# A gated attention and MLP decode step: 832 columns of w2 placed on partitions 0 to 63 by eight small transfers, where 384 columns went to partitions 0 to 15 by four

## The chip, the cores and the metric

The kernel runs on one core of a Trainium2 chip, in one launch. The metric is device microseconds of a whole execution, the median of the runs shown; lower is better. The profile is one further execution, recorded by the hardware profiler, and its own time (its span) is shorter than the timed runs, because the span begins with the first instruction and ends with the last.

## The reference

One decode step for two tokens (B = 2, D = 576). An attention branch A with a KV cache of 4096 positions and 32 heads of 128, an MLP branch with 4608 hidden units and a tanh gelu, and a gate that mixes the two, all in float32:

```python
x = A_x                                               # (2, 1, 576)
g = _sigmoid((x * gate_w).sum(-1, keepdims=True))

q = (x @ wq).reshape(B, 1, 32, 128).transpose(0, 2, 1, 3)
scores = einsum("bhqd,bhkd->bhqk", q, k_cache) * 128 ** -0.5    # k_cache (2, 32, 4096, 128)
p = softmax(scores)
o = einsum("bhqk,bhkd->bhqd", p, v_cache)
a = o.transpose(0, 2, 1, 3).reshape(B, 1, 4096) @ wo            # wo (4096, 576)

h = gelu(x @ w1 + b1)                                 # w1 (576, 4608)
b = h @ w2 + b2                                       # w2 (4608, 576)

out = g * a + (1 - g) * b
```

Nearly all of the 308 MB that is read is the two caches.

## The kernel before, in words

**Storage.** One tile of SBUF, `ring` (128 partitions, three slots of 16,384 words each), takes every large transfer. At the start wq and w1 lie in it; after that slot after slot is refilled in the order k0, v0, k1, v1, ..., k15, v15 (each 8 MB, four heads of one token, 64 KB to each partition) and at the end three mixed loads, the list `LAST`. `load_next` issues the next transfer as soon as the oldest slot is free: a k slot after the scores of it are reduced (the last reader is DVE, `red`; the release is written after `max_n`, L522 in the profile's waits), a v slot after its matmuls (PE, `av`, L551). All of these transfers are issued by SP, strictly in the order of the program. A few small ones (x, gate_w, b1, b2) are issued by ACT.

**The loop.** For each of 16 groups of four heads: DVE multiplies k by the broadcast q (`mul`, L512) and reduces (`red`, L516 on POOL for a part, L517 and L518 on DVE), ACT takes the exponentials (L537), PE multiplies with v (L551), DVE and PE fold the result (L562, L568).

**The tail.** The MLP's second product and the output projection are done at the end. `h` is held as `hg`, 128 partitions by 36 rows, so that partition p, row r is hidden unit 36p + r, and the row r of w2 in the layout "(p r) n" is 128 partitions by 576 columns. `mlp_out(lo, hi)` multiplies rows lo to hi - 1 of it into the accumulator `acc` (`acc_mm`, L371: two products of 288 columns for each row; the profile records each float32 product as two MATMULs). `wo_out` does the same with rows of wo, and `last_out` does rows 23 to 31 of wo into `res` (L463, L487), adds `acc` (L473), copies out and issues the store (L493).

**The columns set apart.** The last 384 of each partition's 36 x 576 words of w2 (the end of row 35) don't lie with the rest on 128 partitions. Before, four transfers (`wx`, L156) put them on partitions 0 to 15: each takes 4 partitions, and each partition receives eight runs of 384 words, which come from eight different partitions p of the layout. `mlp_x` multiplies them with `hx`, a copy of the matching values of `hg` on 16 partitions, made by small products with columns of the identity (L417, L421). `LAST` says which load holds what: rows of w2, the columns set apart (`"wx"`), rows of wo. The last rows of wo come in ever smaller transfers, row 31 in three pieces. The third load is seven transfers in all, the last before the store.

**Order of completion counters.** In the program as built, the transfers use eight completion counters in turn (SP's and ACT's together), and a transfer whose counter is still in use waits at its issue until the transfer eight places before it has landed.

Of the kernel before, what the change touches and what calls it, by code (L numbers as in the profile page):

```python
# [8 lines left out]
F32 = mybir.dt.float32  # L9
# [10 lines left out]
def kernel(  # L20
# [14 lines left out]
    nc = tc.nc  # L35
    B, H, SK, DH = k_cache.shape
    D = x.shape[-1]
# [16 lines left out]
    F4 = F // NG  # L54
# [3 lines left out]
    NF = F // P  # L58
# [5 lines left out]
    SLOTS = 3  # L64

    LAST = (
        (("w2", 0, 14), ("w2", 14, 28)),
        (("w2", 28, 36), ("wx", 0, 1), ("wo", 0, 15)),
        (("wo", 15, 23), ("wo", 23, 27), ("wo", 27, 30), ("wo", 30, 31), ("wo", 31, 32)),
    )  # L70
    FOLD = 23
    SLOT = R * DH
# [8 lines left out]
    cp = ctx.enter_context(tc.tile_pool(name="cp", bufs=1))  # L81
# [8 lines left out]
    ps_sm = ctx.enter_context(tc.tile_pool(name="ps_sm", bufs=3, space=bass.MemoryType.PSUM))  # L90
# [8 lines left out]
    kt, vt, wqt, w1t, rows = {}, {}, {}, {}, {}  # L99
# [22 lines left out]
    def slot(n):  # L122
        k = len(held) % SLOTS
        return ring[:, k * SLOT:k * SLOT + n]
# [7 lines left out]

    srcs = {"w2": w2.rearrange("(p r) n -> p (r n)", r=NF), "wo": wo.rearrange("(p r) n -> p (r n)", r=32)}

    XE, XC, XW = 4, 4, 384
    XL = D - XW
    XP = XE * XC
    XS = P // XP
    srcx2 = w2.rearrange("(e c s r) n -> c r e s n", e=XE, c=XC, s=XS)[:, NF - 1, :, :, XL:]

    def length(w, a, z):
        return XS * XW if w == "wx" else (z - a) * D - (XW if (w, z) == ("w2", NF) else 0)

    def load_last(m):
        n = sum(length(*q) for q in LAST[m])

        used["e"], used["z"] = len(held) % SLOTS * SLOT + n, (len(held) % SLOTS + 1) * SLOT
        t = slot(n)
        o = 0
        for w, a, z in LAST[m]:  # L150
            if w == "wx":
                xt = t[:XP, o:o + XS * XW]
                rows[w] = xt.rearrange("p (s n) -> p s n", s=XS)
                o += XS * XW
                for c in range(XC):
                    nc.sync.dma_start(xt[c::XC].rearrange("e (s n) -> e s n", s=XS), srcx2[c])  # L156
                continue
            if (w, z) == ("w2", NF):
                nc.sync.dma_start(t[:, o:o + length(w, a, z)], srcs[w][:, a * D:z * D - XW])
                for r in range(a, z):  # L160
                    rows[w, r] = t[:, o + (r - a) * D:o + min((r - a + 1) * D, length(w, a, z))]
                o += length(w, a, z)
                continue

            ends = (a * D, a * D + DS, a * D + DS + DO, z * D) if (w, z) == ("wo", 32) else (a * D, z * D)
            for u, v in zip(ends, ends[1:]):
                nc.sync.dma_start(t[:, o:o + v - u], srcs[w][:, u:v])
                o += v - u
            for r in range(a, z):
                rows[w, r] = t[:, o - (z - r) * D:o - (z - r - 1) * D]  # L170

    def temp(n, parts=P):
        t = ring[:parts, used["t"]:used["t"] + n]
        used["t"] += n
        assert used["t"] <= SLOTS * SLOT
        return t
# [7 lines left out]
    def load():  # L184
        if not seq:
            return
        kind, i = seq.pop()
        if kind == "wq":
            wqt[i] = load_w(wq, ROWS[kind], i)
        elif kind == "w1":  # L190
            w1t[i] = load_w(w1, ROWS[kind], i)
        elif kind == "k":
            kt[i] = load_heads(k_cache, i)
        elif kind == "v":
            vt[i] = load_heads(v_cache, i)
        else:
            load_last(i)
        if kind in ("k", "v", "last"):
            held.append((kind, i))
# [7 lines left out]
    xg = temp(D, B + 1)  # L207
# [8 lines left out]
    def load_b1(ends):  # L216
        to, src = b1r.rearrange("(g q) n -> g q n", g=NG)[:, B], b1.rearrange("(g n) -> g n", g=NG)
        for u, v in zip(ends, ends[1:]):
            nc.scalar.dma_start(to[:, u:v], src[:, u:v])


    load_b1((0, 232))
    for b in range(B):
        nc.scalar.dma_start(xg[b:b + 1], x[b])
    nc.scalar.dma_start(xg[B:B + 1], gate_w[None, :])
    load()
    load()
# [2 lines left out]
    ident = cp.tile([P, P], F32, name="ident")  # L230
# [9 lines left out]
    for j in range(NPB):  # L240
        t = cp.tile([P, NT * 32 + EB], F32, name=f"p{j}")
# [71 lines left out]
    for m, ps in enumerate(qps):  # L313
        nc.scalar.copy(qrow[:, m * 512:(m + 1) * 512], ps)
    nc.scalar.dma_start(b2r, b2[None, :])
    load_b1((232, 464, 696, 928, F4))

# [44 lines left out]
    def acc_mm(lhsT, rhs, k, start=False, stop=False, lo=0):  # L364
        m = lhsT.shape[-1]
        hi = lo + rhs.shape[-1]
        for s in range(NS):
            o = 64 * (k % 2) + 32 * s
            u, v = max(lo, s * DS), min(hi, (s + 1) * DS)
            if u < v:  # L370
                nc.tensor.matmul(  # L371
                    acc[o:o + m, u - s * DS:v - s * DS], lhsT, rhs[:, u - lo:v - lo],
                    start=start, stop=stop, skip_group_check=True,
                )
# [28 lines left out]
    hg = cp.tile([P, NF, B], F32, name="hg")  # L403
    t = temp(NF * B).rearrange("p (r b) -> p r b", b=B)
# [7 lines left out]

    load()

    hxps = ps_sm.tile([XP, XS, B], F32, tag="sm", name="hxps")
    for s in range(XS):
        nc.tensor.matmul(  # L417
            hxps[:, s], ident.rearrange("p (q s) -> p s q", s=XS)[:, s], hg[:, NF - 1], start=True, stop=True
        )
    hx = cp.tile([XP, XS, B], F32, name="hx")  # L420
    nc.scalar.copy(hx, hxps)  # L421

    def mlp_x():
        for s in range(XS):
            acc_mm(hx[:, s], rows["wx"][:, s], s, lo=XL)

    def mlp_out(lo, hi):
        for r in range(lo, hi):
            acc_mm(hg[:, r], rows["w2", r], r)
# [14 lines left out]
    def wo_out(lo, hi):  # L444
        for r in range(lo, hi):
            acc_mm(oP[:, :, r], rows["wo", r], r)
# [178 lines left out]
    o_turn(turn)  # L625
    mlp_out(20, 24)
    mlp_x()
    mlp_out(24, NF)
    wo_out(0, FOLD)
    last_out()  # L630

# [27 lines left out]
```

## Time and profile before

| | |
|---|---|
| median of 3 runs | 721.66 us (721.61 to 721.81) |
| span of the profiled execution | 719.7 us |
| DVE, PE, POOL, ACT busy | 71%, 31%, 20%, 6% of the span |
| packets of SP's queue (q1) | 7060, 99.2% of the time of 16 DMA engines |
| packets of ACT's queue (q10) | 48, 0.0% |
| packets of instruction loads (q8) | 13, 0.1% |
| bytes moved, mean rate | 308.83 MB, 429 GB/s |
| the four transfers of L156, in SP's queue | issued from 682.39 us on, in 2.84 us |
| PE on them (L371, out of `hx`) | 32 MATMULs, 4.01 us from 698.94 us on |
| the store of the result issued (L493) | 717.46 us |

How to read it: the shares of busy time are means over the whole span, and the kernel has an opening (projections), a loop and a tail with different limits. The DMA share of a window is the mean over 16 DMA engines of the time that their packets took; over short windows it swings around 1, so that only a lasting fall says that some of the engines have run out of work. PEclk is the granted clock of TensorE, 1.0 or 0.5 here.

### The profile page before, as it was taken

What the parts mean: (1) busy time and instruction counts of PE and PEld (TensorE: products, weight loads), DVE (VectorE), ACT (ScalarE), POOL (GpSimd) and SP (SyncE); (2) the same over time, 40 slices, a digit from 0 to 9 for tenths busy, and PEclk for the clock granted to TensorE, in tenths of its full rate; (3) what the DMA queues carried; (4) which work ended last, traced back from release to release, by engine and by line L of the source; (5) the groups of instructions that cost most, each with busy time, mean ns of one, the idle gap of its engine ahead of it and who ended that gap; (6) DMA issues with size and microseconds to landing.
All of it is one profiled execution on the core that took longest, in us unless ns stands there. A gap on an engine that the chain in (4) does not pass through costs nothing.

```text
span 719.7 us, 3913 instructions
## 1 busy us (share of the span) xinstructions
PE 223.4 (31%) x1663; PEld 66.1 (9%) x1663; DVE 512.0 (71%) x137; ACT 40.0 (6%) x156; POOL 145.0 (20%) x35
## 2 busy tenths in 40 slices
PE   0675022040514050404133140405060503214198
PEld 0321000010101010101000010101010100000024
DVE  0004969779695969596969879696959695988910
ACT  0110010100001010101010100001010101010000
POOL 2000130404050403022040404040403122040400
PEclk9967557565757575655756575757565665657588
DMA  9999999999999999999999999999999999999997
GB/s 408 412 443 434 426 444 419 455 416 455 416 444 428 426 441 430 438 430 444 430 434 426 441 430 437 431 433 437 437 434 441 423 431 437 430 441 431 420 424 308
DMA packets 7126, 308.83 MB, mean 429 GB/s; under 512 B 810, under 2 KB 1342, under 8 KB 1604
## 3 DMA queue, kind: packets, MB, share of 16 engines
q1 hardware_dynamic: 7060, 308.55, 99.2%
q8 instruction: 13, 0.21, 0.1%
q14 instruction: 5, 0.04, 0.0%
q10 hardware_dynamic: 48, 0.03, 0.0%
HBM read 308.57 MB, written 0.00 MB: 429 GB/s over the span
## 4 chain that ended last, share of the span: by engine, by line
DMA 45%; DVE 35%; PE 17%; ACT 1%; issue 1%; ACTq 0%; POOL 0%; DVEq 0%; POOLq 0%
DMA ring<-in_A_k_cache_dram 39%; DVE ring L512 19%; PE av L551 10%; DVE s L517 10%; DVE s L518 5%; DMA ring<-in_B_w_dram 4%; PE acc L371 3%; DMA ring<-in_gate_w_dram 3%; PE oall L568 2%; PE qps L304 1%; DVE avs L562 1%; PE res L463 0%; ACT p L537 0%; DVE m L522 0%; PE zps L280 0%
## 5 line engine op out<-in xcount | busy, mean ns | idle before, releaser
L512 DVE TENSOR_TENSOR ring<-ring,q 128x16384 f32<-128x16384 f32 x16 | 275.6, 17225 | 110.1 <-DMA ring<-in_A_k_cache_dram 110.1
L516 POOL TENSOR_TENSOR ring<-ring 128x3968 f32<-128x3968 f32 x16 | 137.0, 8565 | 491.3 <-DVE ring L512 491.3
L551 PE MATMUL av<-ring,p 128*32 128x512 f32 x1024 | 141.6, 715 | 167.6 <-ACT p L537 167.6
L517 DVE TENSOR_REDUCE s<-ring 128x66 f32<-128x8448 f32 x16 | 143.2, 8953 | 1.3
L568 PE MATMUL oall<-avs,pick 128*64 128x512 f32 x16 | 14.8, 1028 | 195.1 <-DVE avs L562 167.7
L518 DVE TENSOR_REDUCE s<-ring 128x62 f32<-128x3968 f32 x16 | 68.4, 4277 | 0.1
L551 PEld LDWEIGHTS av<-ring,p 128*32 128x32 f32 x1024 | 36.0, 129 | 278.8 <-issue 220.6
L537 ACT ACTIVATE p<-s,bs 32x128 f32<-32x128 f32 x64 | 25.5, 398 | 479.9 <-DVE bs L531 478.7
L352 PE MATMUL qb<-qm,spread 64*128 64x512 f32 x8 | 8.3, 1138 | 71.4 <-POOL qm L348 71.4
L395 DVE TENSOR_TENSOR ring<-hps,ring 128x384 f32<-128x384 f32 x3 | 1.7, 559 | 32.2 <-PE hps L304 32.0
L371 PE MATMUL acc<-ring,hg 128*2 128x288 f32 (+1 forms) x142 | 14.4, 561 | 25.3 <-DMA ring<-in_B_w_dram 25.3
L568 PEld LDWEIGHTS oall<-avs,pick 128*64 128x64 f32 x16 | 2.2, 196 | 201.9 <-DVE avs L562 201.9
L284 DVE TENSOR_SCALAR gb<-gb 128x2 f32<-128x2 f32 x1 | 0.2, 169 | 24.4 <-ACT gb L283 24.4
L483 DVE COPY ring<-res 2x144 f32<-2x144 f32 x1 | 0.3, 296 | 19.3 <-PE res L463 19.3
L304 PE MATMUL hps<-ring 128*32 128x384 f32 x120 | 12.8, 596 | 0.0
L562 DVE TENSOR_TENSOR avs<-av,selr 128x512 f32<-128x512 f32 x8 | 5.5, 682 | 10.1 <-PE av L551 10.1
L348 POOL TENSOR_TENSOR qm<-qall,mine 64x512 f32<-64x512 f32 x4 | 4.1, 1035 | 40.3 <-ACT qall L331 40.3
L537 ACT ACTIVATION_READ_ACCUMULATOR p<-s,bs 32x1 f32 x64 | 11.8, 184 | 0.0
L304 PE MATMUL qps<-ring 128*32 128x512 f32 x80 | 10.7, 697 | 0.0
L271 PE MATMUL xps<-ident,ring 3*128 3x3 f32 x10 | 1.5, 254 | 23.8 <-DMA ring<-in_gate_w_dram 22.8
L352 PEld LDWEIGHTS qb<-qm,spread 64*128 64x128 f32 x8 | 2.0, 308 | 74.5 <-POOL qm L348 74.5
L354 ACT COPY q<-qb 128x512 f32<-128x512 f32 x4 | 2.3, 585 | 106.3 <-PE qb L352 106.3
(88 smaller groups left out, 79.5 us busy)
## 6 DMA issues: line engine op xcount, KB each, us to landing
ring<-in_B_w_dram SPq DMA_DIRECT2D x2, 4608.0 KB, 34.3
ring<-in_B_w_dram SPq DMA_DIRECT2D x2, 4032.0 KB, 28.6
ring<-in_A_wo_dram SPq DMA_DIRECT2D x1, 4320.0 KB
ring<-in_A_wo_dram SPq DMA_DIRECT2D x1, 2304.0 KB, 22.4
ring<-in_B_w_dram SPq DMA_DIRECT2D x1, 2112.0 KB
ring<-in_B_w_dram SPq DMA_DIRECT2D x1, 1152.0 KB
ring<-in_A_wo_dram SPq DMA_DIRECT2D x1, 1152.0 KB
ring<-in_A_wq_dram SPq DMA_DIRECT2D x1, 1024.0 KB
```

The costliest lines, as they stand in the source:

```text
L304: nc.tensor.matmul(ps[32 * j:32 * j + 32, :width], lhs, ts[c][:, o:o + width], start=(k == 0), stop=last, skip_group_check=True,)
L348: nc.gpsimd.tensor_mul(t, qall.unsqueeze(1).to_broadcast([NO, NQ, DH]), mine[:, u[0]:u[-1] + 1].unsqueeze(2).to_broadcast([NO, NQ, DH]),)
L352: nc.tensor.matmul(ps, spread, t.rearrange("p u d -> p (u d)"), start=True, stop=True)
L371: nc.tensor.matmul(acc[o:o + m, u - s * DS:v - s * DS], lhsT, rhs[:, u - lo:v - lo], start=start, stop=stop, skip_group_check=True,)
L512: nc.vector.tensor_mul(kt[i], kt[i], qs[i].unsqueeze(1).to_broadcast([P, R, DH]))
L516: nc.gpsimd.tensor_add(t[:, :, :DH2], t[:, :, :DH2], t[:, :, DH2:])
L517: nc.vector.tensor_reduce(st[i][:, HALVED:], kt[i][:, HALVED:], AX.X, ALU.add)
L518: nc.vector.tensor_reduce(st[i][:, :HALVED], t[:, :, :DH2], AX.X, ALU.add)
L537: nc.scalar.activation(p[w, :, e * RB:(e + 1) * RB], st[i][w].rearrange("p (t c) -> p t c", c=RB), AF.Exp, bias=bias[i][w], accum_out=rs[w ...
L551: nc.tensor.matmul(ps[32 * j:32 * j + 32], p[:, 32 * t + EB * (1 - half):32 * t + EB * (1 - half) + 32], vt[i][:, RB * t:RB * (t + 1)].rea ...
L562: nc.vector.tensor_mul(t, avs[i].rearrange("p (r d) -> p r d", d=DH), selr.unsqueeze(2).to_broadcast([P, RB, DH]))
L568: nc.tensor.matmul(oall, pick[:, NO - G - i * G:2 * NO - G - i * G], avs[i].rearrange("p r d -> p (r d)"), start=(i == 0), stop=(i == N // ...
```

## The change

Three things change.

- **832 columns instead of 384.** The columns set apart are now the last 832 words of each partition (the last 256 columns of row 34 and the whole of row 35). They go to partitions 0 to 63 in two halves of 32 partitions (`XH = 2`), each half in four transfers (`XC = 4`) of 8 partitions (`XE = 8`); every partition receives two runs of 832 words (`XS = 2`), placed 1024 words apart (`XT`). `hx` has 64 partitions and is made by two products instead of eight; `mlp_x` has three products for each of the two runs instead of two for each of eight. The products on row 35 in `mlp_out` go, those on row 34 have 320 columns.
- **Order of the last loads.** The first half goes out after w2's rows 0 to 13, the second after rows 14 to 23, both in the first of the three last loads; rows 24 to 35 (less 832 words) and rows 0 to 15 of wo are the second load; the third begins at row 16 of wo.
- **Small transfers of ACT.** x's two rows come in one transfer, and b1 in four pieces (232, 308, 308 and 304 columns of each of four groups) instead of five.

```diff
     LAST = (
-        (("w2", 0, 14), ("w2", 14, 28)),
-        (("w2", 28, 36), ("wx", 0, 1), ("wo", 0, 15)),
-        (("wo", 15, 23), ("wo", 23, 27), ("wo", 27, 30), ("wo", 30, 31), ("wo", 31, 32)),
+        (("w2", 0, 14), ("wx", 0, 1), ("w2", 14, 24), ("wx", 1, 2)),
+        (("w2", 24, 36), ("wo", 0, 16)),
+        (("wo", 16, 23), ("wo", 23, 27), ("wo", 27, 30), ("wo", 30, 31), ("wo", 31, 32)),
     )
...
-    XE, XC, XW = 4, 4, 384
-    XL = D - XW
-    XP = XE * XC
+    XE, XC, XH, XR, XL = 8, 4, 2, 2, 320
+    XQ = XE * XC
+    XP = XH * XQ
     XS = P // XP
-    srcx2 = w2.rearrange("(e c s r) n -> c r e s n", e=XE, c=XC, s=XS)[:, NF - 1, :, :, XL:]
+    XW = XR * D - XL
+    XT = 1024
+    srcx2 = w2.rearrange("(s h e c r) n -> h c e s (r n)", s=XS, h=XH, e=XE, c=XC)[:, :, :, :, NF * D - XW:]
...
             if w == "wx":
-                xt = t[:XP, o:o + XS * XW]
-                rows[w] = xt.rearrange("p (s n) -> p s n", s=XS)
-                o += XS * XW
+                if a == 0:
+                    rows[w] = t[:XP, o:o + XS * XT].rearrange("p (s n) -> p s n", s=XS)[:, :, :XW]
                 for c in range(XC):
-                    nc.sync.dma_start(xt[c::XC].rearrange("e (s n) -> e s n", s=XS), srcx2[c])
+                    nc.sync.dma_start(rows[w][a * XQ + c:z * XQ:XC], srcx2[a, c])
+                o += length(w, a, z)
                 continue
...
-    for b in range(B):
-        nc.scalar.dma_start(xg[b:b + 1], x[b])
+    nc.scalar.dma_start(xg[:B], x.rearrange("b s d -> (b s) d"))
     nc.scalar.dma_start(xg[B:B + 1], gate_w[None, :])
...
-    load_b1((232, 464, 696, 928, F4))
+    load_b1((232, 540, 848, F4))
...
-    hxps = ps_sm.tile([XP, XS, B], F32, tag="sm", name="hxps")
+    hxps = ps_sm.tile([XP, XS, XR, B], F32, tag="sm", name="hxps")
     for s in range(XS):
         nc.tensor.matmul(
-            hxps[:, s], ident.rearrange("p (q s) -> p s q", s=XS)[:, s], hg[:, NF - 1], start=True, stop=True
+            hxps[:, s], ident[:, s * XP:(s + 1) * XP], hg[:, NF - XR:], start=True, stop=True
         )
...
     def mlp_x():
         for s in range(XS):
-            acc_mm(hx[:, s], rows["wx"][:, s], s, lo=XL)
+            for r in range(XR):
+                lo, u, v = XL * (r == 0), r * D - XL * (r > 0), (r + 1) * D - XL
+                acc_mm(hx[:, s, r], rows["wx"][:, s, u:v], s + r, lo=lo)
...
     mlp_x()
-    mlp_out(24, NF)
+    mlp_out(24, NF - XR + 1)
```

More of the change, by code (lines that the diff above doesn't have):

```diff
@@ L133 @@
     srcs = {"w2": w2.rearrange("(p r) n -> p (r n)", r=NF), "wo": wo.rearrange("(p r) n -> p (r n)", r=32)}
-    XE, XC, XW = 4, 4, 384
-    XL = D - XW
-    XP = XE * XC
+    XE, XC, XH, XR, XL = 8, 4, 2, 2, 320
+    XQ = XE * XC
+    XP = XH * XQ
     XS = P // XP
-    srcx2 = w2.rearrange("(e c s r) n -> c r e s n", e=XE, c=XC, s=XS)[:, NF - 1, :, :, XL:]
+    XW = XR * D - XL
+    XT = 1024
+    srcx2 = w2.rearrange("(s h e c r) n -> h c e s (r n)", s=XS, h=XH, e=XE, c=XC)[:, :, :, :, NF * D - XW:]
     def length(w, a, z):
-        return XS * XW if w == "wx" else (z - a) * D - (XW if (w, z) == ("w2", NF) else 0)
+        if w == "wx":
+            return XS * XT if a == 0 else 0
+        return (z - a) * D - (XW if (w, z) == ("w2", NF) else 0)
     def load_last(m):
@@ L159, in load_last @@
                 nc.sync.dma_start(t[:, o:o + length(w, a, z)], srcs[w][:, a * D:z * D - XW])
-                for r in range(a, z):
+                for r in range(a, z - XR + 1):
                     rows[w, r] = t[:, o + (r - a) * D:o + min((r - a + 1) * D, length(w, a, z))]
@@ L413 @@
     load()
-    hxps = ps_sm.tile([XP, XS, B], F32, tag="sm", name="hxps")
+    hxps = ps_sm.tile([XP, XS, XR, B], F32, tag="sm", name="hxps")
     for s in range(XS):
         nc.tensor.matmul(
-            hxps[:, s], ident.rearrange("p (q s) -> p s q", s=XS)[:, s], hg[:, NF - 1], start=True, stop=True
+            hxps[:, s], ident[:, s * XP:(s + 1) * XP], hg[:, NF - XR:], start=True, stop=True
         )
-    hx = cp.tile([XP, XS, B], F32, name="hx")
+    hx = cp.tile([XP, XS, XR, B], F32, name="hx")
     nc.scalar.copy(hx, hxps)
```

## The prediction

> **What bounds the kernel now.** I read the page's shares and DMA queues first, then the chain that ended last, then the tail in windows of half a microsecond, then what SP waited for.
>
> ```profile
> span 719.7 us, 3913 instructions
> DMA  9999999999999999999999999999999999999997
> GB/s 408 412 443 434 426 444 419 455 416 455 416 444 428 426 441 430 438 430 444 430 434 426 441 430 437 431 433 437 437 434 441 423 431 437 430 441 431 420 424 308
> DMA packets 7126, 308.83 MB, mean 429 GB/s; under 512 B 810, under 2 KB 1342, under 8 KB 1604
> q1 hardware_dynamic: 7060, 308.55, 99.2%
> q8 instruction: 13, 0.21, 0.1%
> q10 hardware_dynamic: 48, 0.03, 0.0%
> ```
>
> The 16 DMA engines are busy in every slice but the last, SP's queue alone fills 99.2% of their time, and no slice between the second and the last falls out of the swing between 416 and 455 GB/s. The kernel is a stream of 308.83 MB at 429 GB/s, 26.8 GB/s for each engine (429/16). The chain says DMA 45% and names DVE and PE for much of the rest, but it goes through them only because a finished slot releases the next transfer; that transfer then stands in a queue that already has work. So a microsecond of compute taken out of the loop is worth nothing, and a byte is worth its time on the engine that ends last. What the change touches is which engine carries which byte. That matters at one place only, where the queue runs dry:
>
> ```profile
> 712.50:713.00 0.50, 0.50 (x15) 0.36 (x10) 0.00 (x0) 0.00 (x0) 0.00 (x0) 1.00 1.02 411
> 713.00:713.50 0.50, 0.50 (x13) 0.19 (x10) 0.00 (x0) 0.00 (x0) 0.00 (x0) 1.00 0.93 366
> 713.50:714.00 0.50, 0.50 (x14) 0.21 (x14) 0.00 (x0) 0.00 (x0) 0.00 (x0) 1.00 0.82 333
> 714.00:714.50 0.50, 0.50 (x22) 0.40 (x22) 0.00 (x0) 0.34 (x1) 0.00 (x0) 1.00 0.67 259
> 714.50:715.00 0.50, 0.50 (x22) 0.40 (x18) 0.00 (x0) 0.07 (x1) 0.00 (x0) 1.00 0.69 259
> 715.00:715.50 0.50, 0.50 (x17) 0.24 (x15) 0.00 (x0) 0.00 (x0) 0.00 (x0) 1.00 0.62 218
> 715.50:716.00 0.50, 0.50 (x27) 0.38 (x18) 0.00 (x0) 0.00 (x0) 0.00 (x0) 1.00 0.48 159
> 716.00:716.50 0.50, 0.50 (x20) 0.19 (x12) 0.00 (x0) 0.00 (x0) 0.00 (x0) 1.00 0.20 61
> ```
>
> The last three columns are the granted clock, the DMA share and GB/s. The share goes down in steps, from 1.02 over 0.82 and about 0.67 to 0.48 and to nothing: about four engines are done near 713.7, four more near 715, and eight work until about 716.3. Their idle part from 713.0 on is half a microsecond times (0.07 + 0.18 + 0.33 + 0.31 + 0.38 + 0.52 + 0.80), 1.3 us as a mean over the engines. So even a perfect levelling ends the stream only 1.3 us (0.18%) sooner. That is the ceiling for every rearrangement of the same bytes.
>
> What follows the last byte is on the path:
>
> ```profile
> 715.25 0.84 PEld L463 LDWEIGHTS res<-ring,oP 128*2 128x2 f32 x32 [0.23 <-DMA ring<-in_A_wo_dram]
> 716.32 0.10 PEld L463 LDWEIGHTS res<-ring,oP 128*2 128x2 f32 x4 [0.23 <-DMA ring<-in_A_wo_dram]
> 716.55 0.48 PE L487 MATMUL res<-ring,oP 128*2 128x72 f32 x8
> 717.46 0.29 SPq L493 DMA_DIRECT2D out_dram<-ring  x1
> ```
>
> PE waits 0.23 us for wo twice at the very end, so it is there before the data: the landings set the end. After them come eight short products (0.48 us), two copies and the store, and none of these changes.
>
> **The change, part by part.**
>
> *The bytes by engine.* The packet count says how many engines a small transfer uses. By the code q1 has 48 transfers on 128 partitions (5 of wq and w1, 32 of k and v, 3 of w2, 8 of wo); with 128 runs and 16 completions each they make 6912 packets, the store makes 4, and 7060 leaves 144 for the four transfers of L156, 36 for each: 32 runs and 4 completions. A transfer on four partitions is carried by four engines; I take eight engines for eight partitions. The columns now set apart are 384 x 4 B x 128 = 196,608 B, so 49,152 B for each of four engines, while all 16 are spared 12,288 B. After the change 832 columns are 425,984 B, 53,248 B for each of eight engines, and all 16 are spared 26,624 B. If the four are among the eight, the difference is:
> - the four that had x already: 4,096 - 14,336 = -10,240 B, at 26.8 GB/s -0.38 us;
> - four further engines: 53,248 - 14,336 = +38,912 B, +1.45 us;
> - the other eight: -14,336 B, -0.53 us.
>
> [...]
>
> All hangs on when the four further engines end now. If they are the four done near 713.7, they end near 715.2, the others at 716.3 less 0.38 or 0.53, and the stream is 0.38 to 0.53 us shorter. If they are those done near 715, they end near 716.4 and nothing is gained. If they are among the eight that end last, the stream ends 1.45 us later. I take the first: the engines are equally loaded by the large transfers, so the spread comes from what only some of them carry, x's runs (1.8 us of bytes on four) and instruction loads (13 of them), and engines that carry neither must be the first to stop. I take 0.45 us. The run lengths work for it a little: 16 runs of 3,328 B and 8 completions on an engine instead of 32 of 1,536 B and 4; I cost that at nothing, between 0.1 us gained and 0.4 us lost (short runs are dearer: 0.48 of the engines moved 159 GB/s, 331 at full share, where 1.02 moved 411).
>
> *PE in the tail.*
>
> ```profile
> 698.94 4.01 PE L371 MATMUL acc<-ring,hx 16*2 16x96 f32 x32
> 702.88 5.17 PE L371 MATMUL acc<-ring,hg 128*2 128x288 f32 x43
> ```
>
> `mlp_x` has 16 products, 32 records at 0.125 us; it will have 6 products, 12 records. Row 35's product (2 records at 0.12 us) goes, row 34 still makes two. That is 20 x 0.125 + 2 x 0.12 = 2.7 us less PE time. It is off the path, for PE waits for wo at 715.25 and 716.32 already. These waits grow by about the 2.7 us less the 0.45 us that the data come sooner; so it is worth 0, and would be worth up to 2.7 us if the landings did not cover it. What could take something back is the clock: the products behind the last landing ran at 1.0, and a PE that waits more might be granted 0.5. Its price lies between 0 and 0.48 us, once more the length of the L487 group; I take 0. The two products for `hx` (eight before) and its copy lie near 66 us, under a full queue: 0.
>
> *SP's queue.*
>
> ```profile
> 651.58 3.76 SPq L167 DMA_DIRECT2D ring<-in_B_w_dram  x2
> 681.63 0.33 SPq L159 DMA_DIRECT2D ring<-in_B_w_dram  x1
> 682.39 2.84 SPq L156 DMA_DIRECT2D ring<-in_B_w_dram  x4
> SPq L159 <- DVE m L522: 26.5, 1, 26.5
> 651.58 28.59 DMA ring<-in_B_w_dram
> ```
>
> The eight small transfers take 0.71 us each to issue (2.84/4), 5.7 us, and now go out from 651.6 on, where SP otherwise waits 26.5 us for the k slot (L159 <- DVE). The counters, eight in turn, add waits: the sixth x transfer stands eight places behind v15, the seventh behind w2's first piece, which landed at 680.2 (651.58 + 28.59), v15 about 9.6 us before (4,128,768 B at 429 GB/s). So x's sixth goes out near 670.7, the seventh and eighth at 680.2 to 681.6, and behind them w2's rows 24 to 35 near 681.6, as now. The engines meanwhile have w2's rows 14 to 23 (2,949,120 B, 6.9 us) from 680.2 at the latest, until about 687. Cost 0, with some 4 us of cover; beyond that, each microsecond of delay is one at the end.
>
> *ACT's small transfers.*
>
> ```profile
> 3.52 19.15 DMA ring<-in_gate_w_dram
> 27.98 8.96 PE qps L304 x64
> 36.96 33.41 DMA ring<-in_A_k_cache_dram
> SPq L130 <- PE qps L304: 1.0, 1, 1.0
> ```
>
> gate_w is the last of three one-partition transfers on an engine that is also loading wq in runs of 64 KB, 2.4 us each (65,536 B at 26.8 GB/s). With x in one transfer, one row and its completion leave that engine's queue: up to 4.9 us (two turns) off the 19.15, and PE's first products come some 4 us sooner. Worth 0: k0's issue waited only 1.0 us for them, and k0 then stood 33.41 us in a queue that was busy throughout. Ends: 0, and 1.0 us gained. One b1 transfer less is 8 packets less on q10, no time.
>
> The sum for this execution is 719.7 - 0.45 = 719.2 us. The timed median of 721.66 us stands 2.0 us above the span, by what lies around it, and I keep that: 721.2 us.
>
> **The rivals.**
>
> *It doesn't show.* The shorter tail is lost to dearer runs (0.4 us), to a slower clock behind the last landing (up to 0.48 us) or to one engine that an instruction load happens to hit. For it: 0.45 us is small beside each of these. Against it: runs of 3,328 B are longer than before, and the granted clock is 1.00 in all the windows shown. Time: 721.6 us. [...]
>
> *The further four engines are not early.* Then +1.45 us falls on engines that end late, and the last byte comes 0.1 to 1.45 us later: 722.6 us, at most 723.1. For it: no row names an engine. Against it: the steps of the share, as above.
>
> *Slower: x's issue waits, and the queue runs dry.* The change moves the small transfers ahead of w2's second piece, into a place where the k slot beside theirs is still being read, until 681.6. The framework orders by the addresses of strided patterns, and one wait in the trace looks like a needless one of this kind:
>
> ```profile
> ACT ring L620 <- DMA ring<-in_B_w_dram: 10.3, 1, 10.3
> ```
>
> L620 writes words of another slot, and yet waited 10.3 us until the four x transfers had landed. If the first x transfer in the same way waits for the readers of k15, it goes out at 681.6, and w2's second piece behind four issues (2.84 us) at 684.5, its data a microsecond later. The engines have nothing after w2's first piece, from 678 to 680 on: 5 to 7 us dry, 727.7 us. It decides from the point where x's first issue comes after about 679. Against it: large contiguous patterns show no such wait, nor did PE's reading of v15 wait for x.
>
> *Faster by the start.* If PE's earlier start counted after all, up to 4 us would go: 717.5 us. Against it: the full queue.
>
> **How the numbers follow.** Forecast 0.62; doesn't show 0.22; further four not early 0.06; dry queue 0.06; start 0.04. The predicted time is the forecast's, 721.2 us. The forecast and the first rival hold 0.84: from 721.66 less 0.53 and less the 0.1 us for longer runs and 0.3 us for levelling that I have undersized, 720.7, up to 721.66 plus 0.3 for a loss that exceeds the gain, 722.0. A measurement of this kernel can tell about 0.2%, 1.44 us, from no change: 720.2 to 723.1. Only the start makes it faster than that, 0.04; the dry queue and the worst end of "not early" make it slower, 0.08; the same, 0.88.
>
> **What would show it.** Right: q1 with 7108 packets (6912 + 8 x 24 + 4) and q10 with 40; L156 eight times in SP's queue between 651 and 682; `hx` with 12 MATMULs; PE's waits for wo in the tail well above 0.5 us in total; the DMA share staying near 1 until about 715 and then falling at once; the store some 0.45 us sooner. Wrong: a DMA share below 0.9 between 676 and 690 (dry queue); a share of about 0.25 for more than a microsecond before the last landing (four engines too late); a clock of 0.5 in L487.

## The result and the profile after

The changed kernel takes 723.15 us (median of 21 runs, 722.24 to 724.63), the kernel before 721.65 us (721.53 to 722.03): a ratio of 1.002, 95% interval 1.0014 to 1.0026. The forecast was 721.2 us, the upper end of the range 722.0 us. Two things have changed about the times: the median is 1.5 us higher, and the spread is 2.4 us where it was 0.5. Three executions of the runs below, of 738.93, 751.22 and 1135.31 us, fell into a slower state and are left out.

The profiled execution has a span of 721.0 us. The page's first lines, with DMA queues as before:

```profile
span 721.0 us, 3846 instructions
DMA  9999999999999999999999999999999999999996
q1 hardware_dynamic: 7108, 308.55, 99.1%
q8 instruction: 13, 0.21, 0.1%
q10 hardware_dynamic: 40, 0.03, 0.0%
```

The packet counts are those forecast, 7108 and 40. The tail in the same half-microsecond windows (last three columns: granted clock, DMA share, GB/s):

```profile
714.50:715.00 0.50, 0.46 (x16) 0.42 (x20) 0.00 (x0) 0.00 (x0) 0.00 (x0) 1.00 0.87 343
715.50:716.00 0.50, 0.45 (x16) 0.11 (x5) 0.00 (x0) 0.00 (x0) 0.00 (x0) 1.00 0.57 206
716.00:716.50 0.50, 0.00 (x0) 0.00 (x0) 0.00 (x0) 0.00 (x0) 0.00 (x0) 1.00 0.39 134
716.50:717.00 0.50, 0.41 (x16) 0.36 (x20) 0.00 (x0) 0.00 (x0) 0.00 (x0) 1.00 0.20 68
717.00:717.50 0.50, 0.50 (x28) 0.30 (x16) 0.00 (x0) 0.00 (x0) 0.00 (x0) 1.00 0.12 40
```

Up to 715 the engines are better levelled than before (0.87 where it was 0.69). Then the share doesn't fall at once: 0.20 and 0.12 are three and two engines of 16 that are still at work after 716.5, when before all were done (a share of 0.00 there). PE's timeline (start, duration, instructions, in brackets its idle time before them) shows what that costs, and SP's the store:

```profile
714.54 1.16 PE L468 MATMUL res<-ring,oP 128*2 128x144 f32 x32 [0.65 <-DMA ring<-in_A_wo_dram]
716.59 1.54 PE L468 MATMUL res<-ring,oP 128*2 128x144 f32 x36 [0.65 <-DMA ring<-in_A_wo_dram]
717.92 0.51 PE L492 MATMUL res<-ring,oP 128*2 128x72 f32 x8
718.86 0.29 SPq L498 DMA_DIRECT2D out_dram<-ring  x1
```

PE waits for rows 27 to 29 of wo until 716.59, where it began on them at 715.25 before: 1.34 us later, and the store goes out 1.40 us later (718.86 against 717.46). So the loss shows at the end; it has two causes, and one of them lies at the other end of the trace. It shows in ACT's copies of the identity, PE's products on q and on the hidden units (`hps`), and SP's issue of v0, first in the kernel before:

```profile
41.09 0.89 ACT L323 COPY ring<-ident 128x8 f32<-128x8 f32 x8 [1.83 <-DMA ring<-in_B_b_dram]
41.35 3.06 PE L329 MATMUL qps<-ring 128*64 128x128 f32 x16 [2.75 <-ACT ring L323]
49.84 12.76 PE L304 MATMUL hps<-ring 128*32 128x384 f32 x120
60.03 0.33 SPq L130 DMA_DIRECT2D ring<-in_A_v_cache_dram  x1
```

and in the kernel after:

```profile
36.80 1.61 ACTq L223 DMA_DIRECT2D ring<-in_B_b_dram  x3
47.82 0.90 ACT L326 COPY ring<-ident 128x8 f32<-128x8 f32 x8 [10.70 <-DMA ring<-in_B_b_dram]
48.08 3.67 PE L332 MATMUL qps<-ring 128*64 128x128 f32 x16 [11.63 <-ACT ring L326]
57.17 11.69 PE L307 MATMUL hps<-ring 128*32 128x384 f32 x120
66.30 0.33 SPq L130 DMA_DIRECT2D ring<-in_A_v_cache_dram  x1
```

ACT issues the later pieces of b1 and then makes copies that have nothing to do with b1. Before, they follow the last issue at once (the 1.83 us are ACT's own issuing). After, they wait 10.70 us, for the landing of the three pieces: in the trace the first copy waits for three counters more than before, those of the three pieces. With it PE's products on q start 6.7 us later, though gate_w landed 2.6 us sooner, and v0 goes out at 66.30 instead of 60.03. By then k0's data are nearly through. The windows around it, before and then after:

```profile
65.00:67.50 2.50, 0.00 (x0) 0.00 (x0) 1.96 (x9) 0.26 (x1) 0.00 (x0) 0.69 0.91 393
67.50:70.00 2.50, 0.69 (x16) 0.61 (x16) 0.50 (x4) 0.16 (x1) 0.00 (x0) 0.50 1.03 446
```

```profile
65.00:67.50 2.50, 2.50 (x36) 0.94 (x32) 0.00 (x0) 0.00 (x0) 0.00 (x0) 1.00 0.97 419
67.50:70.00 2.50, 1.36 (x20) 0.26 (x12) 2.15 (x4) 0.00 (x0) 0.00 (x0) 1.00 1.15 426
```

A share of 1.15 for 426 GB/s, where before 1.03 carried 446, says that the packets take longer. In the trace the first packets of v0, 64 KB each, take 2.5 to 3.4 us where nearly all others take 2.418: here engines that ran dry started again together, as they did at the very beginning of both kernels (2.5 to 3.4 us there too). Counted over the packets, the engines idle by 0.10 us as a mean around 68.5 us, and the 64 KB packets up to 130 us take 0.6 us more as a mean than at 2.418 each. Together this prices the late v0 at 0.7 us in the profiled execution.

### The profile page after: what moved, and what is told of

The parts are those of the page before. It is cut to its first block, busy times and chain, and to the rows that moved or that the text cites. A ratio compares the mean times of both kernels' runs of the same rounds, so it can differ in the third digit from the quotient of the medians.

```text
span 721.0 us, 3846 instructions
## 1 busy us (share of the span) xinstructions
PE 217.8 (30%) x1629; PEld 63.4 (9%) x1629; DVE 511.9 (71%) x137; ACT 40.0 (6%) x156; POOL 145.0 (20%) x35
## 3 DMA queue, kind: packets, MB, share of 16 engines
q1 hardware_dynamic: 7108, 308.55, 99.1%
## 4 chain that ended last, share of the span: by engine, by line
DMA 45%; DVE 35%; PE 15%; ACT 2%; issue 1%; ACTq 0%; POOL 0%; DVEq 0%; SPq 0%; POOLq 0%
DMA ring<-in_A_k_cache_dram 34%; DVE ring L517 19%; DVE s L522 10%; PE av L556 9%; DVE s L523 5%; DMA ring<-in_B_w_dram 4%; DMA ring<-in_A_wo_dram 4%; DMA ring<-in_gate_w_dram 2%; ACT p L542 2%; PE hps L307 2%; PE qps L307 2%; DMA ring<-in_B_b_dram 1%; PE acc L374 1%; PE qps L332 1%; DVE m L527 0%
## 5 line engine op out<-in xcount | busy, mean ns | idle before, releaser
L556 PE MATMUL av<-ring,p 128*32 128x512 f32 x1024 | 137.1, 696 | 161.8 <-ACT p L542 161.8
```

Of the source, the lines that this page charges most:

```text
L556: nc.tensor.matmul(ps[32 * j:32 * j + 32], p[:, 32 * t + EB * (1 - half):32 * t + EB * (1 - half) + 32], vt[i][:, RB * t:RB * (t + 1)].rea ...
```

## The experiments

Two theories stood against each other. R: ACT's copy waits, v0 is late, the queue runs dry. L: some of the engines that now carry the columns of w2 also serve PE's instruction loads, and so end last. Both turned out to hold, and the runs part them.

**ACT's part alone**, on the kernel before (b1's pieces and x's transfer as after, w2 as before):

```diff
-    for b in range(B):
-        nc.scalar.dma_start(xg[b:b + 1], x[b])
+    nc.scalar.dma_start(xg[:B], x.rearrange("b s d -> (b s) d"))
...
-    load_b1((232, 464, 696, 928, F4))
+    load_b1((232, 540, 848, F4))
```

> The kernel before with the change on ACT's queue alone (x in one transfer, b1 in four pieces). Theory L (two of the eight engines that now carry x's columns are also among those that PE's instruction loads go to, 13 loads of 16 KB, so they end last): no part of it is here, 721.65 us, at most 0.2 us off. Rival S (the earlier start of PE shifts the stream, and that is the loss): 723.1 us, as the whole change.

Measured: 722.72 us (721.94 to 723.75) beside 721.71, ratio 1.0015 (1.0006 to 1.0024). About 1.0 us of the loss is ACT's part, which I had costed at nothing; theory L as the only cause was wrong. Its trace has the late v0 and the long packets:

```profile
65.94 0.33 SPq L130 DMA_DIRECT2D ring<-in_A_v_cache_dram  x1
67.50:70.00 2.50, 1.00 (x16) 0.12 (x4) 2.30 (x4) 0.00 (x0) 0.00 (x0) 1.00 1.25 426
```

**b1 in five pieces again**, all else as after, and **w2's part alone** (ACT's transfers all as before):

```diff
-    load_b1((232, 540, 848, F4))
+    load_b1((232, 464, 696, 928, F4))
```

> The kernel after with b1 in five pieces as before (232, 232, 232, 232, 224 columns); all else of the change stays. Theory R (with pieces of 304 to 308 columns ACT's copy of the identity waits for their landing, 10.7 us; q, hps and with them v0's issue come 6 us later, at 66.3 us, when k0's data end at 67.6, and the 16 engines run dry and start again together): the copy starts near 39 us, v0 goes out at 60 us or sooner, no gap between 60 and 70 us, and what is left is the forecast for w2's part, 721.2 us (720.7 to 721.8). Theory L (instruction loads on engines that carry x's columns): at most the 1.0 us that ACT's part alone cost goes, 722.1 to 722.4 us.

> The kernel after with all of ACT's transfers as before (x in two, b1 in five); only the 832 columns, the order of the last loads and hx change. Theory R: 721.2 us (720.7 to 721.8), no gap near 67 us. Theory L: 722.1 to 722.4 us, with the last landings on a few engines at 717 us as in after.

**Four pieces, the wide one first**, so that the three later ones are narrow:

```diff
-    load_b1((0, 232))
+    load_b1((0, 456))
...
-    load_b1((232, 540, 848, F4))
+    load_b1((456, 688, 920, F4))
```

> The kernel after, b1 still in four pieces, but the first, which is issued at the start, takes 456 columns and the three later ones 232 each (after: 232, then 308, 308, 304). Theory R in its narrow form (it is the width of the later pieces that makes the copy wait, not their number): as with five pieces, the copy starts near 39 us, v0 at 60 us, 721.2 us (720.7 to 721.8). If the number of pieces or the shift of the completion counters were the cause: 723 us, as after.

In all three the copy no longer waits for b1, and v0 goes out at 56.08, 57.40 and 54.94 us. Rows of the one with 456 columns first:

```profile
38.32 0.90 ACT L326 COPY ring<-ident 128x8 f32<-128x8 f32 x8 [1.34 <-DMA ring<-in_B_b_dram]
54.94 0.33 SPq L130 DMA_DIRECT2D ring<-in_A_v_cache_dram  x1
```

So it is the width of the later pieces that makes the copy wait (232 columns don't, 304 to 308 do), not their number: theory R in its narrow form. (Where the pieces begin changes with their width; no run parts these two.) The times fall into two groups in each kernel, with nothing between 721.56 and 722.53:

| kernel | median | lower group | upper group | ratio to before |
|---|---|---|---|---|
| five pieces | 722.79 | 3 runs, mean 721.45 | 8 runs, mean 722.86 | 1.0009 (1.0000 to 1.0018) |
| w2's part alone | 722.82 | 3 runs, 721.50 | 8 runs, 722.88 | 1.0009 (1.0001 to 1.0018) |
| 456 first | 721.38 | 6 runs, 721.26 | 5 runs, 722.61 | 1.0001 (0.9992 to 1.0010) |

The kernel before, on the same chip, has one group, 721.53 to 722.31 with a median of 721.83. In the lower group the forecast of 721.2 us is met within 0.3 us, and the gain over the kernel before on this chip is 0.33 to 0.57 us where 0.45 was forecast. The upper group is 1.35 to 1.41 us above the lower one. The same two groups are in a fourth kernel, the one with 456 columns first with the last rows of wo cut otherwise (`("wo", 23, 28), ("wo", 28, 30)`):

> As the kernel with 456, 232, 232 and 232 columns of b1, and the last rows of wo cut otherwise: 23 to 27 and 28 to 29 in one transfer each, where after has 23 to 26 and 27 to 29. A candidate: after has PE wait for rows 27 to 29 at 716.59 and then work 2.0 us without a pause, some 0.4 us past the last landing; one row less behind that landing is 8 records, 0.34 us. Gain 0 to 0.3 us against the kernel without it; if PE then has too much behind rows 23 to 27, a loss of up to 0.3 us.

Measured: 722.65 us, 3 runs at 721.31 and 8 at 722.69 as means, so no gain in either group. Its profiled execution was one of the upper group (span 720.8), that of the kernel with 456 columns first one of the lower (719.5). Their tails, the lower first:

```profile
716.00:716.50 0.50, 0.50 (x18) 0.14 (x8) 0.00 (x0) 0.00 (x0) 0.00 (x0) 1.00 0.19 54
716.50:717.00 0.50, 0.45 (x12) 0.14 (x8) 0.30 (x1) 0.27 (x1) 0.00 (x0) 1.00 0.00 0
```

```profile
716.00:716.50 0.50, 0.50 (x25) 0.39 (x19) 0.00 (x0) 0.00 (x0) 0.00 (x0) 1.00 0.09 32
716.50:717.00 0.50, 0.50 (x24) 0.38 (x16) 0.00 (x0) 0.00 (x0) 0.00 (x0) 1.00 0.07 25
717.00:717.50 0.50, 0.50 (x16) 0.11 (x8) 0.00 (x0) 0.00 (x0) 0.00 (x0) 1.00 0.06 21
```

A share of 0.06 to 0.07 is one engine of 16: it works alone for more than a microsecond, from about 716.2 on. What delays it can be read by following the packets in the trace. It doesn't name their engines, but on one engine each packet starts within nanoseconds of its predecessor's end. A load of PE's instructions (16,384 B) took 0.93 us in these traces, and the 64 KB packet behind it 2.91 us instead of 2.418: 1.42 us together (1.42 to 1.44 for every such pair between 70 and 590 us in eight traces), the distance of the two groups. Followed so, the 13 loads of each of these executions go to eight different engines in turn; those hit first, in these kernels at about 36 and 56 to 68 us, are hit again at about 612 and 655 us. The engines with columns in five profiled executions, with times from the start of the span as in the views:

```
profiled execution     span   engines with columns that were hit (end of their load), and the end of the last of these
after                  721.0  536.4 us; 614.0 us, a second hit    717.74 us
cut otherwise          720.8  611.5 us, a second hit              717.62 us
five pieces            719.7  458.1 us; 535.1 us                  716.35 us
w2's part alone        719.7  380.6 us; 457.9 us                  716.21 us
456 first              719.5  303.4 us; 380.4 us                  716.26 us
```

In these five, two engines of the eight with columns are neighbours in the round of loads. Which of the 13 fall on them differs between executions; in the first two it is one of the first (36 to 37 us in after), and that engine is hit twice. This following is not certain everywhere (engines whose packets end in the same nanosecond can be exchanged).

The loads' own durations say the same without it. Up to 660 us, in every trace with 13 loads, two neighbours of the round take 0.88 to 0.89 us and the other six 0.92 to 0.97, and the ninth load begins the round again: in the kernel after, loads 1 to 5 take 0.888, 0.938, 0.931, 0.922 and 0.962 us, loads 9 to 13 take 0.888, 0.934, 0.933, 0.924 and 0.958. In the kernels of the table the two short ones are those that lead to columns. They stand at places 8 and 1 of the round in the first two executions of the table, which end at 717.6 to 717.7 us, and at places 7 and 8, 6 and 7, and 5 and 6 in the other three. Places 1 to 4 come again as loads 9 to 12, ahead of the end; the second load of place 5 begins only at 716 us or later. The loads were then tried by themselves.

**Fewer instruction loads.** Three quarters of the products of p and v are left out (so the kernel computes something else), first in the kernels before and after, later in the one with 456 columns first:

```diff
-        for t in range(NT):
+        for t in range(NT // 4):
...
-                stop=(half == 1 and t >= NT - 4),
+                stop=(half == 1 and t >= NT // 4 - 4),
```

> The kernel before with three quarters of the products of p and v left out (8 of 32 for each v slot; v is loaded in full), so that PE's instructions are about half as many and its 13 instruction loads become about 7, one for an engine at most. Theory L: the end is set by the four engines with x and by PE's own work, which stay: 721.3 to 721.6 us. It is there to be compared with the next.

> The kernel after with the same three quarters of the products of p and v left out, about 7 instruction loads of PE instead of 13. Theory L: the engine with x that was hit twice is hit once at most, 1.4 us less: 721.3 to 721.8 us, within 0.3 us of the same cut in the kernel before, where the two whole kernels are 1.5 us apart. Rivals B (too many bytes on the further engines), S (the start) and W (PE's waits for the last landings): none of them hangs on the instruction loads, and the 1.5 us between the two stay.

> The kernel with 456, 232, 232, 232 columns of b1 (no gap near 67 us), and in it three quarters of the products of p and v left out (8 of 32 for each v slot; v is loaded in full): 7 instruction loads of PE instead of 13. Theory L (the loads go round eight engines in turn; two neighbours among these carry x's columns; with 13 loads the first engines of the round are hit again, and where that falls on one of the two the time is 1.4 us longer): no engine is hit twice, so the slower of the two groups of times, about 722.65 us, is gone; all runs between 721.0 and 721.7 us. Rival C (the two groups come from something that the loads don't touch, such as the order in which the engines start): both groups stay, 1.3 to 1.4 us apart.

The page of the last has

```profile
q8 instruction: 7, 0.11, 0.1%
```

Measured: 721.59 us (721.48 to 721.87) for the kernel before, 721.96 us (721.43 to 722.51) for after, 721.38 us (721.09 to 722.08) with 456 first. With 7 loads the upper group is gone: nine of eleven runs of the last lie between 721.09 and 721.58, two at 721.90 and 722.08. In the kernel after, where the queue still runs dry, the 1.5 us shrink to 0.4. That is theory L's second half; the two runs above 721.7 are more than it allowed (in the profiled execution loads still hit engines with columns at 691 and 710 us). The edit takes away PE's work as well as its loads; that the loads are what counts rests on this run and the places in the round together.

**ACT's part mended, w2 as before** (x in one transfer; b1 with 456, 232, 232, 232):

> The kernel before with x in one transfer and b1 in four pieces of 456, 232, 232 and 232 columns; w2 as before. Theory R: ACT's copy doesn't wait, no gap near 67 us, and nothing is left of the 1.0 us that ACT's part alone cost: 721.65 us, 0.2 us to either side. Theory L: x's columns lie on engines that no load of PE hits, so there is one group of times only. If PE's 2 us earlier start counted, it would show here: 719.7 us.

Measured: 721.85 us (721.70 to 721.93), one group, ratio 1.0002 (0.9993 to 1.0011); v0 goes out at 55.17. So the 1.0 us of ACT's part is its wait, and the start, with k0 issued at 34.26 instead of 36.96 us, is worth nothing.

**Six engines instead of eight.** If the two engines that are hit are not among those that transfers of 6 partitions use, six would do. That these are six engines is my estimate from the completion packets (4 for a transfer to 4 partitions before, 8 for one to 8 after); that they leave out the two was a guess. Six kernels tried it, five of which lost for another reason first. The first, ten transfers of 6 partitions and one of 4:

```diff
-                for c in range(XC):
-                    nc.sync.dma_start(rows[w][a * XQ + c:z * XQ:XC], srcx2[a, c])
+                for g in groups[:XG // 2] if a == 0 else groups[XG // 2:]:
+                    nc.sync.dma_start(rows[w][g], srcx2[g])
```

with `groups` of the partitions c, c + 10, ..., c + 50 and the four left over.

> The kernel after, the same 832 columns to the same partitions 0 to 63 with the same runs, but in ten transfers of 6 partitions and one of 4 instead of eight of 8: six engines carry about 71 KB each instead of eight 53 KB. Theory L: the two engines that are hit by instruction loads no longer carry any of it; the six end at 715.1 + 0.66 = 715.5 to 716.1 us, the stream some 1.0 us before the 717.1 us of after: 721.6 to 722.1 us, and the runs lie closer together than the 722.2 to 724.6 of after. Rival B (the bytes on the further engines are too many, whichever these are): 0.66 us more on each, 723.8 us.

Measured: 727.45 us (725.09 to 728.02). Rows 24 to 35 of w2 went out late, since three more small transfers stood ahead of them, the last six of the eleven taking 10.89 us to issue, with one wait of 6.6 us for a landing of w2:

```profile
685.05 0.35 SPq L166 DMA_DIRECT2D ring<-in_B_w_dram  x1
```

instead of at 681.96 us. Between 660 and 700 us the engines idle by 0.15 us as a mean, where after has 0.02; most of the loss is something else, which comes out below. Two more have the columns on 32 partitions and only rows 0 to 19 of w2 in the first load:

> A candidate: 704 columns (instead of 832) of w2 on partitions 0 to 31, four runs each 1024 words apart, in five transfers of 6 partitions and one of 2; rows 20 to 35 of w2 and 0 to 12 of wo in the second load; b1 with 456, 232, 232, 232 columns. Theory L: only the six engines that no load of PE hits carry them, one group of times, 721.2 to 721.5 us, 0.3 to 0.5 us faster than before. Rival B (six engines with 56 to 68 KB each become the last): 721.9 us or more. [...]

> As the candidate with 704 columns, with 832: 67 to 80 KB on each of the six engines. Theory L: one group of times; the two engines with 80 KB end about 0.35 us later than with 704 columns, 721.3 to 721.8 us.

Measured: 724.6 and 725.76 us. They issue rows 20 to 35 at 681.8 and 682.0 us, and with four rows less ahead of them (4 x 294,912 B, 2.7 us at 429 GB/s) the engines idle by 0.70 and 0.65 us as a mean. That is not the whole of the 3 and 4 us lost; how the rest divides was not followed. The window in the first of them, with share and rate both low:

```profile
680.00:685.00 5.00, 4.77 (x54) 1.57 (x57) 2.47 (x4) 1.96 (x8) 0.00 (x0) 0.65 0.91 336
```

Then transfers of six with the order mended (five ahead of rows 14 to 23, two behind them, four behind rows 24 to 35):

> A candidate: the kernel after with 456, 232, 232, 232 columns of b1, and the 832 columns on partitions 0 to 63 in ten transfers of 6 partitions and one of 4, of which five go out ahead of w2's rows 14 to 23, two behind them and four behind rows 24 to 35, so that the issue of rows 24 to 35 waits for no small transfer and the first load keeps its 24 rows. Theory L: only six engines carry the columns and none of these is hit by PE's loads: one group of times, 721.2 to 721.6 us; 0.2 to 0.5 us faster than before. Rival C: two groups 1.3 us apart, as with eight engines. Rival B (71 KB are too many for six engines): one group, 722 us or more.

> The same with 704 columns: 56 to 62 KB on each of the six engines, 4 KB more on all 16. Theory L: one group, 721.1 to 721.5 us; better than with 832 if the six engines are the last, worse by 0.15 us if the engines with two loads are.

Measured: 725.20 us (724.38 to 726.82) and 724.36 us (723.63 to 726.19), with no engine idle between 660 and 700 us, but with longer packets (runs of 112 to 352 ns, large ones of up to 1.7 us where 0.855 to 1.194 is usual). So the distance of the partitions was tried, on eight engines and by itself (8 apart instead of 4; b1 with 456, 232, 232, 232):

```diff
-                    nc.sync.dma_start(rows[w][a * XQ + c:z * XQ:XC], srcx2[a, c])
+                    nc.sync.dma_start(rows[w][a * XC + c::XE], srcx2[a, c])
```

> The kernel with eight engines and 456, 232, 232, 232 columns of b1 (721.38 us), with one thing changed: a transfer's eight partitions lie 8 apart instead of 4 (the same 64 partitions, the same bytes). Theory S4: its runs of 3,328 B take longer than the 131 ns of after, the packets behind them too, and the time is 723.5 us or more. If the distance makes no difference, 721.1 to 722.7 us in two groups.

Measured: 727.40 us (725.59 to 727.50), ratio 1.0067 (1.0054 to 1.0080). The two groups are there too, two runs with a mean of 725.67 and three with 727.45, each 4.4 to 4.8 us above its own with four apart. Windows of it, and then of the same kernel with partitions four apart:

```profile
676.00:681.00 5.00, 0.00 (x0) 0.00 (x0) 4.87 (x2) 0.00 (x0) 1.40 (x1) 0.50 0.97 306
686.00:691.00 5.00, 5.00 (x64) 1.63 (x59) 0.00 (x0) 0.00 (x0) 0.00 (x0) 1.00 1.02 331
```

```profile
676.00:681.00 5.00, 0.79 (x8) 0.25 (x12) 4.89 (x2) 0.00 (x0) 1.58 (x1) 0.50 0.98 420
686.00:691.00 5.00, 5.00 (x52) 1.44 (x48) 0.00 (x0) 0.38 (x1) 0.00 (x0) 1.00 0.98 422
```

The share is full in both, the rate a quarter less in the first. In the trace the runs of 3,328 B take 201 ns in the median and up to 325, where all of them take 131 with four apart, and the large packets of w2 behind them up to 1.75 us where nearly all take 0.855 or 0.902 with four apart. With that known, six engines with partitions four apart:

> A candidate: as the last (704 columns, b1 with 456, 232, 232, 232 columns), but the six engines' partitions lie four apart in each transfer, as the eight's do in after (partitions 0 to 23 with three runs, 32 to 55 with two, 768 words apart; 8 left over in one transfer), where the two kernels with six engines that lost had them ten apart. In those two no engine idled (0.00 us a mean between 660 and 700), yet their 128 runs took 112 to 352 ns where the shortest is 112, and the large packets behind them up to 1.7 us instead of 0.855 to 1.194. Theory S4 (partitions that aren't four apart make engines collide): that goes, and theory L is tried at last: one group of times, 721.1 to 721.5 us, 0.2 to 0.5 us faster than before. If six engines are too few for it, 722 us or more; if loads hit these six too, two groups.

Measured: 722.92 us, ratio 1.0011 (1.0003 to 1.0020): 5 runs with a mean of 721.86 and 6 with 723.13. The runs of 2,816 B take 112 ns (115 at most; 131 x 2,816/3,328 is 111), but there are two groups again. In its profiled execution, one of the lower group, one of the six engines with columns can be followed to a load at 455 us. It is one of the two with the short duration (0.88 us), at place 7 of the round. So theory L's guess at which engines are free of loads was wrong; that loads make the two groups is not refuted, but that six engines would end them is. No kernel that was run beats the one before clearly: the best, with 456 columns first, is 0.6 us faster in its lower group (721.26 against 721.83 on the same chip), and even in the ratio.

## Why the prediction was wrong

The step that failed first is *ACT's small transfers*: "One b1 transfer less is 8 packets less on q10, no time", and "PE's first products come some 4 us sooner. Worth 0". I had asked what hides k0's issue and had found it; I did not ask who else stands behind b1's pieces. The copy stands right behind them on ACT, and the wider pieces made it wait 10.70 us; v0, not k0, was the transfer that went out too late. Price: 722.72 us with the wait against 721.85 without (act_only and act_early), 0.9 us; the two ran on different chips, and against the kernel before on each it is 0.8 us. What makes it worse is that the idea was in the prediction: the wait of L620 (10.3 us), taken for a needless one that the framework puts in by the addresses of strided patterns, which was my reading and which no run shows as such. I applied it to x's first transfer alone, not to the strided transfers of b1, whose size the change altered.

The second step that failed is *the bytes by engine*. That engines with neither x's runs nor instruction loads stop first fits the runs, but I took the four further engines to be these as a block. That a transfer to eight partitions is carried by eight engines fits the packets, 24 for each (16 runs and 8 completions, 6912 + 8 x 24 + 4 = 7108). That the four of before are among the eight, on which the 0.38 and 0.53 us behind the 0.45 us rest, was assumed, and no run shows it. What the runs showed in its place is that two of the eight are in the round of the instruction loads. Hit once, such an engine ends at 716.2 to 716.35 us, not near 715.2 as I had it, so it is as late as the rest and has no room for a second load. Where their loads come once, the forecast holds as a time (721.26 to 721.50 as means of the lower groups; 721.2 forecast), in part by luck. In these traces the last landing is at 716.26 to 716.35 us, hardly sooner than the 716.35 before, so the 0.45 us that I put on it isn't seen there, and where the lower groups gain their 0.33 to 0.57 us stays open.

Where one is hit twice, it is the rival *the further four engines are not early*, to which I gave 0.06: 722.61 to 722.88 us, where I had 722.6. Together, as means: 721.65, less 0.3 as in the lower groups, plus 1.4 in two of three runs (29 of the 44 in the four kernels with two groups and no dry queue), plus 0.7 (after against five pieces, a mean of 722.48) to 1.0 (ACT's part alone) for the dry queue, is about the 723.15 us.

The page of after has 13 loads of 16,384 bytes for 3,258 instructions of PE, that of the kernel with 456 columns first and fewer products 7 for 1,722: one for 251 and one for 246. A load cost the DMA engine that carried it 1.42 us in these traces.

The other steps. *What bounds the kernel*: right for the stream, but "the landings set the end" was misread. The two waits of 0.23 us are PEld's; PE itself waits for no transfer after 690 us in the trace before. In the chain of waits it works without a pause from 697.2 us on:

```profile
697.20 16.57 PE acc L371 x173
713.76 0.13 PE res L463 x3
```

PE ends at 717.03 (716.55 + 0.48), 0.7 us behind the last packets (716.35). So in the kernel before PE's own work, too, sets the end.

*PE in the tail*: `hx` has 12 records, and the 2.7 us came back as PE's waits for wo, 2.5 us in all, as said. But "worth 0" doesn't follow: by the trace before, data that land 0.45 us sooner would have found PE still at work, so the shorter work was a condition of the gain. No run has the one without the other. The clock stayed at 1.0. *SP's queue*: the eight issues lie between 668.55 and 681.53 us, not from 651.6 on, for the first was made to wait for DVE's multiplication of k15:

```profile
SPq L159 <- DVE ring L517: 17.3, 1, 17.3
668.55 3.45 SPq L159 DMA_DIRECT2D ring<-in_B_w_dram  x4
```

That is the needless wait of the rival *the queue runs dry*. It ended some 10 us ahead of the point at which it would have decided, so the rival failed here; but the cover behind it was smaller than the 4 us that I took: an issue 3.1 us later, or 2.7 us less of data ahead of it, was enough for idle engines (0.15 us, and 0.65 to 0.70 us as means, in the first three kernels with six).

## What to carry to other kernels

Where a change alters the size or the stride of a small transfer, look at every instruction behind it on the same queue and see whether its list of waits has changed; one needless wait 40 us into the kernel cost more here (0.7 to 1.0 us) than the change was to gain at the end (0.45 us). When bytes are moved to "other engines", what else these engines carry must be known, instruction loads among them (1.42 us each here); where it isn't, the forecast is two numbers with a chance each, not one with a range.

## What the runs showed of the hardware that I had not expected

An instruction load of PE cost one DMA engine 1.42 us (1.42 to 1.44 for every pair of load and 64 KB packet that was followed). The loads went round eight of the 16 engines in turn (in the kernel after, the durations of loads 1 to 5 and 9 to 13 agree within 4 ns), and the traces show four different starting points of this round. The four kernels with columns on eight engines and no dry queue have two times each, 721.26 to 721.50 and 722.61 to 722.88 us as means.

Transfers whose partitions lie 8 apart made their own packets and those of other transfers longer (the runs 201 ns in the median instead of 131, the large ones up to 1.75 us instead of 0.9), which cost 4.4 to 4.8 us with eight engines; 10 apart, with six, the runs took 112 to 352 ns (four apart 112 to 115 with 704 columns, 131 with 832). Four apart, the runs kept their length in the kernels before and after (65 ns for every run of 1,536 B, 131 for every one of 3,328 B). What makes the difference was not shown: with the partitions, the rows of w2 that are read lie twice as far apart too.

The 16 engines that ran dry and started again together lost more than the gap: in the kernel after, 0.10 us of idle time as a mean, and 0.6 us because the first 64 KB packets take 2.5 to 3.4 us instead of 2.418 and some of the later ones up to 2.9.
